# A hand-written order of 1,700 units of work: loads of two batches reordered, 19 sums on the other engine, a third of the units moved

## The chip, the cores and the metric

The kernel runs on one core of a Trainium2 chip. Its engines are named as in the profile: PE (TensorE: matmuls; PEld is its weight load), DVE (VectorE), ACT (ScalarE), POOL (GpSimd) and SP (SyncE, which here only issues stores). The metric is the device time of one execution in microseconds (us). A measurement is the median of several runs.

## What is computed

The kernel is an attention with 32 memory slots followed by a bilinear feed-forward network. Cut to what matters:

```
q, k, v: (8 batches, 8 heads, 576 tokens, 64)      phi: (8, 8, 576, 32)
a     = softmax over tokens of phi
k_m   = a^T k        v_m = a^T v                    (32 slots x 64, per head)
attn  = softmax over slots of q k_m^T / 8
x     = attn v_m, heads side by side                (4608 tokens x 512)
out   = ((x w_a) * (x w_b)) w_out                   (d_ff = 1536)
```

All arrays are float32 outside; the matmuls inside take float16.

## The kernel before, in words

**What a batch goes through.** phi, k, v and q of a batch are loaded by DMAs that POOL issues (L152, L155, L158, L163), k, v and q being cast to float16 on the way. ACT takes exp of phi (L291); PE sums k and v over the slots (`kv`, L323); DVE scales them (`km`, L350 and L355); PE turns them round (`kvt`, L363). DVE transposes q (`qt`, L300); PE makes the scores (`sc`, L412), ACT their exp (`e`, L425). For batches 0 to 3 the softmax is normalised through logarithms (`den`, `nr`, L465 to L478; for batches 2 and 3 the product L478 is POOL's); for the others by transposing on DVE, summing and multiplying (`ed`, `sm`, `tn`, `ad`, L485 to L506; `tn0` on POOL). The weights w_a and w_b are folded into v_m (`v0a` to `v2b`, eight narrow matmuls each for 512 columns and one weight, L516) and copied from PSUM to SBUF (`x`, L548, mostly ACT). So x w_a is one product of `attn` with the folded weights `vab`.

**The up projection** of a batch is cut into 12 blocks of 128 columns (i) and two halves of 288 tokens (hf; for batch 1 the halves are 320 and 256). A unit `a{b}.{i}.{hf}` is two matmuls and ACT's copy of the result to `a_sb` (L727, L731); `b{b}.{i}.{hf}` is two matmuls and DVE's product of `a_sb` and the second result into `ht` (L727, L734). For some blocks of batches 5, 6 and 7 both halves are made together with seven products in place of eight (`P{b}.{i}.{k}`, one matmul each, L750, L755, L759, L777), with a last product `H` (on POOL) or `J` (on DVE) (L781). These need sums of the folded weights (`S`, L533) and of the attention (`T`, L541), each marked P or D for POOL or DVE.

**The down projection** takes two blocks of 128 tokens together, also in seven products of six matmuls each: 18 pairs of 42 steps `d` (one matmul each, L654). It needs four sums of `ht` per pair, `h{pair}.{y}` on POOL or `g{pair}.{y}` on DVE (L638). ACT takes three partial results (L661) and one output (L705), DVE adds the rest (L665), and SP stores (L644).

**PSUM** has eight banks. The class `Banks` (from L198) gives each new result the bank that was freed longest ago; PE has to wait until ACT or DVE has read the result that lay there.

**The order** is written out by hand in the string `PLAN` (L18 to L80), a list of units. The last loop of the kernel (L785 on) walks through it and issues each unit's instructions; a scheduler does not reorder them. Each engine runs its own instructions in the order of the list, and semaphores hold it where data or a buffer is missing. POOL therefore issues a load only after the sums that stand ahead of it in the list, but it may be far ahead of PE. `d3` means three steps; a load is a letter and a batch: `p` phi, `k`, `v`, `q`, and `wa`, `wb`, `o` for weights. `kv_sb` has two buffers, so batches 4 and 6 take the one of 2; q and phi have two buffers each.

Of the kernel before, what the change touches and what calls it, by code (L numbers as in the profile page):

```python
# [15 lines left out]


PLAN = """  # L18
wb0:256 0qt0 wa0:256 0qt3 wb256:512 0qt1 wa256:512 p1 0exp0 0exp1 F1 0ks0 0kt0 0ks1 0vs1 0vt1 0vs0 0vt0 M k1 F1
0hv0a 0s0 v1 0qt2 O 0kt1 0e0 F1 0s1 0e1 0hx0a0 0hx0a1 F2 0den10 0den01 0den11 0den00 wa512:1024 0hv0b 0hx0b0 0hx0b1  # L20
0hv1b 0nr01 0nr10 0hx1b1 0nr11 0nr00 0hv1a 0hx1a0 q1.0 wb512:1024 0hx1a1 F4 a0.0.1 1exp1 a0.0.0 b0.0.0 0hx1b0 a0.1.1
b0.0.1 1exp0 a0.3.1 b0.1.1 a0.3.0 a0.2.0 b0.3.1 b0.2.0 a0.2.1 b0.2.1 1kv a0.1.0 1km1 wa1024:1536 1km0 b0.3.0 q1.1
1kvt 0v1a 0x1a0 0x1a1 1v0a 1v1a 1v0b 1x1a0 1x0a0 1x0b0 a0.5.1 1x1a1 1qh20 wb1024:1536 b0.1.0 o1 a0.6.0 1qh30 a0.4.0
1qh10 1qh00 o0 o3 1sh0 1eh00 0v1b 1v1b 1x0b1 1eh10 1x0a1 0x1b0 1den00 0x1b1 1x1b1 o4 1den10 o2 a0.6.1 b0.6.0 b0.6.1
b0.5.1 1nr10 1nr00 1x1b0 b0.4.0 a0.7.1 b0.7.1 a0.7.0 a0.5.0 b0.7.0 a1.5.0 b0.5.0 h0.3 b1.5.0 a1.3.0 1qh21 a0.4.1 o5
b1.3.0 1qh31 1qh01 a1.4.0 b0.4.1 a1.1.0 1qh11 a1.2.0 b1.4.0 a1.0.0 b1.1.0 1sh1 0v2a 1eh01 1eh11 0x2a1 b1.0.0 0x2a0
b1.2.0 1den01 a1.6.0 0v2b 0x2b0 0x2b1 b1.6.0 v2 a0.9.1 1v2b 1v2a 1x2b0 1x2b1 a0.11.1 1x2a1 1x2a0 b0.9.1 a0.10.1
a0.9.0 b0.11.1 b0.10.1 b0.9.0 V20 1den11 a1.10.0 b1.10.0 a0.11.0 b0.11.0 a0.8.0 a1.11.0 b0.8.0 b1.11.0 1nr11 d1
1nr01 a0.10.0 d1 V00 a1.8.0 b0.10.0 a1.7.0 d1 b1.8.0 p2 V21 a1.11.1 b1.7.0 b1.11.1 d1 a1.3.1 a1.0.1 a1.2.1 g0.0 d1
b1.3.1 a1.6.1 d1 b1.2.1 b1.0.1 V01 a0.8.1 V10 a1.4.1 a1.9.0 d1 k2 2exp0 2exp1 g0.1 d1 V11 b1.6.1 V31 a1.5.1 p3 g0.2  # L30
b0.8.1 q2 d1 b1.4.1 d3 a1.1.1 b1.9.0 d6 2kv 3exp0 k3 d2 2km0 d1 a1.9.1 2km1 v3 d3 b1.5.1 d1 3exp1 d1 a1.10.1 d2
a1.8.1 2kvt b1.1.1 d2 h1.0 a1.7.1 2qt1 d4 2qt0 2qt3 2v1b 2x1b1 2v0a 2x1b0 T30 2qt2 2x0a1 d12 2x0a0 d4 g2.0 g1.1 2sc
# [6 lines left out]
a2.2.1 d1 q5 d1 4qt0 b2.11.1 4qt3 4exp1 d1 3x0b1 d3 b2.2.1 d1 a2.9.1 d1 4qt1 d2 4qt2 d1 a2.7.1 b2.9.1 g4.3 d1 a2.6.1
h4.0 a2.3.1 d1 g4.1 d1 a3.3.0 d1 h4.2 4exp0 k7 b2.7.1 a3.2.0 d2 b2.6.1 d5 b3.3.0 b3.2.0 d2 4kv p6 3v2a 4km0 d2 3x2a1  # L40
4km1 d11 3x2a0 b2.3.1 d2 4kvt d2 a3.0.0 a3.3.1 v6 5km0 q6 d2 a3.1.0 5km1 k6 h5.0 d5 b3.1.0 a3.1.1 4sc 4e0 b3.0.0 d1
5qt3 d2 b3.1.1 5qt0 d1 a3.0.1 4e1 d3 b3.3.1 d5 3v1b 3v1a 4ed 3v2b 3x1b1 d5 3x1a0 d2 3x1a1 4sm0 d1 5qt1 d2 h5.3 3x2b0
5kvt a3.8.0 4sm1 d1 3x1b0 h5.1 3x2b1 d4 5qt2 d3 a3.6.1 b3.0.1 a3.10.0 d3 a3.4.0 d1 p7 d1 6exp1 d1 b3.8.0 b3.4.0 d1
a3.5.0 b3.6.1 d1 b3.10.0 4tn1 a3.7.0 a3.9.0 h5.2 d1 5sc 4tn0 5e0 d1 b3.5.0 5e1 a3.5.1 a3.11.0 d1 b3.7.0 d3 6qt0 d4
4v0a 4x0a0 4v1b 4v0b 4x0b1 d2 4x1b1 d5 6qt2 d1 4ad d1 5ed d1 a3.4.1 5sm0 b3.5.1 d2 b3.9.0 d1 4x1b0 d3 4x0a1 b3.11.0
d2 q7 d3 6qt1 d1 a3.6.0 a3.2.1 h6.3 6exp0 b3.6.0 d2 b3.4.1 d2 4x0b0 a3.8.1 a3.7.1 d5 a3.11.1 d2 b3.11.1 b3.8.1 d1
5tn0 d2 b3.2.1 4v2b 4v2a 4x2b0 6kv h6.0 4v1a d2 4x2b1 d1 5sm1 4x2a0 6km1 6km0 h6.1 6qt3 d3 b3.7.1 4x1a1 d3 4x1a0
a3.9.1 d2 4x2a1 5tn1 d2 b3.9.1 d3 a3.10.1 a4.0.0 g6.2 a4.2.1 b3.10.1 b4.0.0 d1 a4.3.0 d2 a4.0.1 6kvt b4.2.1 a4.6.0
d5 5ad 5v1a 6sc 5x1a1 h7.3 d1 6e1 d1 5x1a0 d1 7qt0 b4.6.0 d1 6e0 b4.0.1 d6 5T0D d2 h7.0 5v1b 5v0a 5v0b 5x1b0 g7.1
g8.0 g8.3 5x1b1 5T1D g7.2 5x0a0 d3 5x0b0 d6 5x0a1 b4.3.0 d8 5S01D a4.9.1 5T3D v7 a4.7.0 g8.1 b4.7.0 a4.10.1 a4.8.0  # L50
d1 b4.9.1 d1 5x0b1 a4.1.1 d2 5S11D 5S31P b4.8.0 b4.10.1 6ed 5S21P a4.6.1 a4.11.0 d1 b4.6.1 a4.5.0 d1 P5.4.1 7exp0
b4.5.0 b4.11.0 d1 b4.1.1 d3 P5.5.1 P5.4.2 a4.2.0 P5.5.2 d3 5S00P a4.1.0 d1 7qt3 5T2P P5.4.6 a4.9.0 h8.2 d1 a4.4.0
6sm0 d1 P5.5.5 b4.2.0 d1 7exp1 d1 6tn0 d1 b4.9.0 P5.4.5 P5.4.7 d1 P5.5.6 d3 P5.5.3 d1 a4.8.1 d2 b4.1.0 d1 5S10P d1
P5.4.3 P5.4.4 a4.4.1 a4.7.1 5S20P b4.4.1 d2 b4.4.0 d1 b4.8.1 5v2a 7qt2 5v2b 5x2a0 P5.5.7 5x2b0 b4.7.1 d4 5x2a1 6sm1
a4.10.0 a4.3.1 b4.3.1 d2 5x2b1 P5.5.4 P5.1.1 a4.11.1 b4.10.0 h9.3 d1 6tn1 d6 5S30D a4.5.1 d1 P5.2.1 P5.1.6 d1 J5.5
g9.0 a5.10.1 d1 P5.1.5 P5.2.2 d1 b4.11.1 d1 H5.4 h9.1 P5.1.7 d3 P5.1.2 d1 P5.2.5 d2 P5.2.6 d2 P5.1.3 P5.6.1 d1
P5.1.4 d1 P5.2.3 a5.11.0 d1 P5.2.7 d2 P5.7.1 a5.8.0 h9.2 d1 b4.5.1 P5.7.5 P5.6.6 P5.2.4 d3 P5.7.6 d1 P5.6.5 d1
P5.6.2 H5.1 P5.7.3 H5.2 d5 h10.0 P5.7.2 P5.6.7 a5.8.1 P5.3.1 P5.7.7 P5.6.3 b5.11.0 P5.0.1 d3 h10.1 d2 P5.6.4 P5.0.5
P5.3.6 P5.7.4 d1 b5.10.1 P5.0.6 d3 a5.9.0 6ad H5.7 d2 H5.6 P5.0.3 P5.3.2 d1 P5.3.5 d3 P5.0.2 d1 P5.3.7 d2 P5.0.7 d1
h10.3 a5.10.0 d1 P5.3.3 d3 6T0P d1 P5.3.4 d1 P5.0.4 d1 6T1P 6v0a 6x0a0 6x0a1 6T2P 7qt1 7kv 6v2b 6v0b H5.0 7km0 d1  # L60
H5.3 d1 6x2b1 d1 7km1 d4 6x0b0 6x0b1 d1 b5.8.0 6x2b0 d2 6T3P a5.11.1 b5.10.0 7kvt d1 b5.9.0 d3 6S00P d2 6v1a 7sc
6S10D d3 6x1a0 d1 7e1 d1 g11.0 6S30D g10.2 7e0 b5.8.1 6x1a1 d1 b5.11.1 d6 6v2a 7v1a 6v1b 6x2a1 g11.1 d1 6x1b0 6S20D
d2 6x1b1 d4 7ed 7sm0 a5.9.1 d4 6x2a0 d1 b5.9.1 7x1a1 P6.3.1 d7 6S01P d1 P6.3.2 d1 7x1a0 a6.11.0 7sm1 d1 P6.3.5
P6.3.6 d1 h11.2 d2 P6.1.1 d2 P6.1.2 d2 6S11P d1 b6.11.0 a6.8.0 P6.3.3 P6.1.6 P6.3.7 P6.1.5 d1 a6.10.0 d3 P6.2.5 d3
g12.0 6S31P P6.2.1 7tn1 d1 6S21D g11.3 P6.1.3 d4 H6.3 P6.1.7 P6.0.1 d3 P6.2.6 P6.3.4 d1 P6.2.3 d3 P6.0.6 d4 P6.2.2
P6.1.4 P6.2.7 d1 P6.0.5 d3 a6.10.1 d1 H6.1 P6.0.7 d2 P6.6.1 h12.1 d2 P6.2.4 d1 P6.0.3 P6.0.2 P6.6.5 H6.2 d4 h12.2
P6.6.6 d1 7tn0 P6.0.4 b6.8.0 P6.5.1 d2 H6.0 d2 P6.6.3 P6.6.7 d1 a6.9.0 H6.6 P6.6.2 d2 P6.5.6 d1 P6.5.2 P6.4.1
b6.10.0 P6.5.5 P6.6.4 d3 P6.5.7 d1 h12.3 7ad P6.4.5 d1 P6.4.6 d1 P6.5.3 P6.7.1 P6.4.2 d3 P6.5.4 d4 7T2P d1 7T0P
P6.7.6 P6.4.7 P6.4.3 P6.7.5 H6.5 d3 P6.7.2 d4 P6.4.4 d1 H6.4 d1 h13.3 d1 P6.7.3 P6.7.7 7v0a 7v1b 7x0a0 d2 7x1b1
b6.9.0 d1 7x0a1 d2 7x1b0 d1 P6.7.4 d2 7T1D a6.8.1 7S01D g13.0 7S11D a6.11.1 d1 7T3D d1 g13.1 7v0b 7x0b1 J6.7 7v2a  # L70
7v2b 7S21D g13.2 7x2a0 d2 7x2b1 d11 P7.4.1 d3 P7.4.2 7x0b0 b6.10.1 d5 7x2a1 7S31D 7S00D d2 7x2b0 d3 7S10P b6.11.1 d1
P7.4.6 a7.8.0 d2 P7.4.5 d2 b6.8.1 a6.9.1 P7.4.7 P7.7.1 P7.7.5 P7.4.3 d1 b7.8.0 b6.9.1 a7.11.0 d1 P7.4.4 P7.7.6 d1
a7.10.0 P7.7.3 d2 P7.5.1 P7.7.2 d1 7S30P d1 P7.7.7 P7.5.5 d2 H7.4 b7.10.0 P7.5.2 P7.5.6 h14.0 P7.6.1 d2 P7.7.4
a7.9.0 d1 P7.5.3 d2 P7.5.7 d1 J7.7 d1 g14.1 d1 P7.6.6 d1 P7.1.1 P7.6.5 P7.6.2 d1 7S20P d1 h14.2 P7.5.4 d3 P7.6.7
H7.5 d1 b7.11.0 P7.1.6 d1 h14.3 P7.1.5 P7.6.3 d1 P7.1.2 d2 P7.6.4 d1 P7.0.1 d1 P7.1.7 d1 H7.6 d1 b7.9.0 d1 P7.0.5 d1
P7.0.2 d1 P7.1.3 P7.0.6 d2 P7.1.4 P7.2.1 d2 P7.0.3 P7.3.1 d3 P7.0.7 P7.2.2 P7.2.6 P7.3.5 d3 P7.3.6 d2 J7.0 P7.2.5
P7.0.4 d1 H7.1 P7.2.7 d1 a7.10.1 P7.3.7 d5 P7.3.2 d2 P7.2.4 d3 P7.3.4 g15.0 d1 a7.8.1 d3 a7.9.1 g15.1 a7.11.1
# [764 lines left out]
```

## Time and profile before

| | us |
|---|---|
| median of 3 runs | 234.23 |
| lowest and highest run | 233.62 to 234.96 |
| span of the profiled execution, first to last instruction | 232.1 |
| busy in it: PE, DVE, ACT, POOL | 214.1, 195.7, 169.4, 138.2 |

The profile gives of the profiled execution only its span; the runs include what lies around it as well. The TensorE clock was granted in full (1.000). The views used below are: the windows (busy time of each engine in a stretch), the waits (who waited for whom), the timeline of one engine, the chain of work that ended last, the groups of equal instructions, and the DMA issues with their time to landing. Start times count from the start of the span.

### The profile page before, as it was taken

The page shows a single profiled execution, that of the slowest core. Times are in us where ns is not written, and L with a number is a line of the kernel's source. Part 1 is how long each engine was busy: PE and PEld are TensorE (multiplying, and loading weights), DVE is VectorE, ACT ScalarE, POOL GpSimd, SP SyncE. Part 2 cuts the span into 40 slices and gives each one's busy share as a digit, 9 for nine tenths or more (in the row PEclk, how much of TensorE's full clock was granted, in tenths as well). Part 3 has the DMA queues.
Part 4 walks back from the last instruction along what each step waited for, and adds up shares of the span by engine and source line. Part 5 has one row for each costly group of instructions (what it writes and reads, how often), then busy time and mean ns, then how long its engine had stood idle before and what let it go on. Part 6 is the DMA issues. An engine that isn't in the chain of part 4 may idle for free.

```text
span 232.1 us, 7493 instructions
## 1 busy us (share of the span) xinstructions
PE 214.1 (92%) x2906; PEld 163.6 (70%) x2906; DVE 195.7 (84%) x517; ACT 169.4 (73%) x450; POOL 138.2 (60%) x139
## 2 busy tenths in 40 slices
...
GB/s 229 238 199 256 205 205 205 205 259 258 208 284 138 264 207 243 253 241 254 210 93 4 190 1 65 28 64 32 93 3 90 78 16 92 18 77 55 42 158 111
DMA packets 26259, 34.09 MB, mean 147 GB/s; under 512 B 2000, under 2 KB 20304, under 8 KB 26224
## 3 DMA queue, kind: packets, MB, share of 16 engines
...
q1 hardware_dynamic: 5952, 9.70, 16.2%
q10 hardware_dynamic: 512, 0.79, 1.0%
...
q14 instruction: 13, 0.11, 0.1%
...
## 4 chain that ended last, share of the span: by engine, by line
PE 71%; DMA 17%; POOL 6%; ACT 3%; issue 2%; DVE 1%; POOLq 0%
PE py L654 18%; PE pb L727 11%; PE pa L727 11%; PE pv L654 9%; DMA wb_sb<-in_moe_w_b_dram 6%; DMA kv_sb<-in_k_dram 6%; PE py L750 5%; PE px L654 4%; PE pva L516 4%; DMA kv_sb<-in_v_dram 4%; PE pv L750 3%; POOL h_sums L638 2%; PE pkv L323 2%; PE px L750 1%; ACT vab L548 1%
## 5 line engine op out<-in xcount | busy, mean ns | idle before, releaser
L734 DVE TENSOR_TENSOR ht<-a_sb,pb 128x288 f16<-128x288 f16 (+2 forms) x144 | 60.5, 445 | 9.6 <-PE pb L727 5.3
L727 PEld LDWEIGHTS <-vab 128*128 128x128 f16 x576 | 55.3, 98 | 14.9 <-issue 2.4
L731 ACT CAST a_sb<-pa 128x288 f16<-128x288 f32 (+2 forms) x144 | 55.1, 417 | 13.6 <-PE pa L727 8.9
L727 PE MATMUL pb<-A,vab 128*128 128x288 f16 (+2 forms) x288 | 54.9, 286 | 0.1
L727 PE MATMUL pa<-A,vab 128*128 128x288 f16 (+2 forms) x288 | 54.3, 286 | 0.5 <-DVE A L478 0.4
L548 ACT CAST vab<-pva 128x512 f16<-128x512 f32 x82 | 45.4, 611 | 6.9 <-PE pva L516 6.8
L654 PEld LDWEIGHTS <-h_sums 128*128 128x128 f16 x432 | 41.4, 98 | 9.9 <-issue 2.4
L638 POOL TENSOR_TENSOR h_sums<-ht 128x768 f16<-128x768 f16 x19 | 31.2, 1645 | 21.4 <-DVE ht L734 21.3
L654 PE MATMUL py<-w_sums,h_sums 128*128 128x256 f16 x216 | 38.1, 273 | 0.0
L654 PEld LDWEIGHTS <-ht 128*128 128x128 f16 x324 | 31.2, 98 | 7.5 <-issue 2.2
L654 PE MATMUL pv<-wo_sb,h_sums 128*128 128x256 f16 x216 | 36.4, 273 | 0.0
L638 POOL TENSOR_TENSOR h_sums<-ht,h_sums 128x768 f16<-128x768 f16 x10 | 16.4, 1640 | 11.6 <-DVE h_sums L638 11.5
L755 ACT COPY z<-py 128x288 f32<-128x288 f32 x48 | 19.2, 415 | 2.3 <-PE py L750 1.8
L781 POOL TENSOR_TENSOR ht<-ah,bh 128x288 f16<-128x288 f16 x19 | 13.7, 737 | 10.1 <-DVE ah L759 7.1
L654 PE MATMUL px<-wo_sb,ht 128*128 128x256 f16 x108 | 18.9, 273 | 0.0
L654 PE MATMUL py<-wo_sb,ht 128*128 128x256 f16 x108 | 18.8, 273 | 0.0
L654 PE MATMUL py<-w_sums,ht 128*128 128x256 f16 x108 | 18.4, 273 | 0.0
L661 ACT ACTIVATE u<-py 128x256 f32<-128x256 f32 x36 | 14.4, 399 | 4.0 <-PE py L654 3.9
L425 ACT ACTIVATE E<-pscore 128x288 f16<-128x288 f32 x28 | 9.8, 431 | 9.5 <-PE pscore L412 9.4
L291 ACT ACTIVATE exp_sb<-phi_sb 128x576 f16<-128x576 f32 x16 | 10.9, 692 | 5.2 <-DMA phi_sb<-in_phi_dram 5.2
L300 DVE STREAM_TRANSPOSE qT<-q_sb 128x288 f32<-128x288 f32 x28 | 12.2, 456 | 2.6 <-DMA q_sb<-in_q_dram 2.6
L750 PE MATMUL py<-asum,vab 128*128 128x288 f16 x48 | 13.5, 286 | 0.0
...
## 6 DMA issues: line engine op xcount, KB each, us to landing
...
phi_sb<-in_phi_dram POOLq DMA_DIRECT2D x8, 576.0 KB, 10.3
kv_sb<-in_v_dram POOLq DMA_DIRECT2D x8, 576.0 KB, 11.2
kv_sb<-in_k_dram POOLq DMA_DIRECT2D x7, 576.0 KB, 13.5
q_sb<-in_q_dram POOLq DMA_DIRECT2D x6, 576.0 KB, 11.9
wo_sb<-in_moe_w_out_dram POOLq DMA_DIRECT2D x6, 256.0 KB, 14.0
wa_sb<-in_moe_w_a_dram POOLq DMA_DIRECT2D x2, 512.0 KB, 14.2
...
```

Source lines behind the costliest of these rows:

```text
L291: nc.scalar.activation(out=t["exp"][:, 2 * z:2 * z + 2, :, :], in_=phis[b][:, 2 * z:2 * z + 2, :].rearrange("p c (i m) -> p c i m", m=M), ...
L300: nc.vector.transpose(out=t["qT"][:, hp, :].bitcast(F32), in_=qs[b][:, hp, :].bitcast(F32))
L548: engine_copy(out=vabs[b][z][:, g, lo:hi], in_=pva[:, 0:hi - lo])
L638: engine.tensor_tensor(out=out, in0=in0, in1=in1, op=op)
L654: nc.tensor.matmul(po, lhs[:, i], rhs[:, i], start=first and i == 0, stop=i == KH - 1, skip_group_check=not first)
L661: nc.scalar.mul(out=x, in_=po, mul=scale)
L727: nc.tensor.matmul(ps, vabs[b][x][:, g, P * i:P * (i + 1)], attn[b][:, g, ts], start=(g == 0), stop=(g == 1))
L731: nc.scalar.copy(out=a_sbs[b, i, hf][:, :n], in_=ps)
L734: nc.vector.tensor_tensor(out=ht[:, i, t0:t0 + n], in0=a_sbs.pop((b, i, hf))[:, :n], in1=ps, op=ALU.mult)
L750: nc.tensor.matmul(x[bank][0], lhs, rhs, start=first, stop=True, skip_group_check=True)
L755: nc.scalar.copy(out=x[name], in_=po)
L781: engine.tensor_tensor(out=ht[:, i, t0 + HALF:t0 + S], in0=x["ah"], in1=x["bh"], op=ALU.mult)
```

## The change

Only the string `PLAN` changes; no code does. The list has the same units but for the engine of 19 sums, and its first 195 units, each step `d` counted, (to about 49 us) are the same. Behind them:

- **Loads.** The order of issue on POOL from phi of batch 2 on was `p2 k2 p3 q2 k3 v3 q3 p5 v5 p4 k5 q4 v4 k4 q5 k7 p6 v6 q6 k6 p7 q7 v7` and is `p2 k2 p3 q2 v3 k3 q3 p5 q4 p4 k5 v5 v4 k4 q5 p6 q6 p7 k6 v6 k7 q7 v7`.
- **Sums moved from DVE to POOL** (11): g3.1, g4.1; 5S11, 5S30; 5T0, 5T1, 5T3, 7T1; J5.5, J7.0, J7.3.
- **Sums moved from POOL to DVE** (8): h2.2, h3.2, h17.2, h17.3; 5T2, 7T2; H5.4, H6.4.
- **Places.** About a third of the 1,500 units behind the first eighth stand more than 1 us of PE's work earlier or later than before, some 230 of them more than 2 us; the steps `d` stand in fewer and longer groups.

The diff where POOL's loads of batches 3, 5 and 4 stand, and at the end of the list:

```diff
-g1.2 2e0 b1.7.1 d1 2e1 g1.3 q3 d2 b1.8.1 d3 b1.10.1 d1 2den0 d1 g2.1 p5 2den1 d1 b1.9.1 d1 2nr0 d5 2v2b 3kv 2v1a
-g2.3 2x2b1 3km0 2nr1 2x2b0 2x1a1 d7 3km1 d6 3qt2 2x1a0 2v0b 2v2a 2x0b1 3qt3 d3 3qt0 2x2a1 d3 a2.6.0 d1 b2.6.0 d1
-3qt1 a2.4.0 2x2a0 b2.4.0 d1 h2.2 d1 a2.7.0 d2 a2.4.1 d1 2x0b0 b2.4.1 d4 a2.3.0 a2.1.1 3kvt 5exp1 v5 b2.7.0 p4 b2.3.0
-a2.8.0 b2.1.1 k5 a2.1.0 d2 a2.2.0 d2 q4 d1 a2.5.0 h3.3 3sc 3e0 d2 b2.2.0 d1 3e1 d2 b2.8.0 5exp0 d1 b2.1.0 v4 d2
-a2.10.0 d2 b2.10.0 a2.0.1 a2.11.0 b2.11.0 b2.5.0 3den0 a2.0.0 d1 b2.0.1 h3.0 d1 g3.1 a2.5.1 d1 a2.9.0 k4 b2.5.1 h3.2
...
+b1.5.1 a1.4.1 d7 T30 d2 2kv 3exp0 a1.8.1 d3 q3 d1 2km0 d1 2km1 b1.9.0 3exp1 b1.4.1 d2 a1.10.1 d2 a1.9.1 p5 d2 2kvt
+b1.1.1 d1 2qt1 d1 2qt3 d2 a1.7.1 2qt0 2v0a 2x0a0 2v1b 2x1b0 2qt2 d5 2x1b1 d6 b1.10.1 d2 2x0a1 d2 g1.1 d1 2sc 2e0
+b1.7.1 2e1 b1.9.1 d1 q4 d2 g1.2 d5 2den0 g2.0 d3 2den1 g1.3 2nr1 2nr0 d3 g2.3 2v2b 3kv 3km1 3km0 2x2b0 2v1a d6 2x1a0
+d3 p4 d2 2x1a1 d1 k5 d3 v5 2x2b1 2v2a 2x2a0 3qt0 2v0b 2x0b0 2x2a1 v4 b1.8.1 d2 h3.0 h3.1 a2.6.0 d4 b2.6.0 a2.7.0 g2.1
+2x0b1 a2.4.0 b2.4.0 a2.9.0 b2.9.0 a2.5.0 b2.5.0 d1 3qt3 a2.5.1 d2 a2.3.0 d1 a2.1.1 d3 b2.7.0 5exp1 b2.3.0 a2.10.0
+b2.1.1 d2 a2.2.0 h3.3 3qt2 d1 3qt1 d2 5exp0 d1 b2.10.0 a2.4.1 b2.5.1 3kvt a2.0.0 g2.2 a2.8.0 b2.8.0 d3 g3.2 3sc 3e0 k4
...
-b7.11.1 b7.9.1 d12 g15.2 g15.3 P7.2.3 b7.8.1 P7.3.3 d12 b7.10.1 d1 J7.3 H7.2 g16.0 d7 g16.1 g16.2 g16.3 g17.0 g17.1
-d2 h17.2 d20 h17.3 d66
...
+b7.9.1 d2 g15.3 P7.2.3 P7.3.3 d2 a7.11.1 d5 b7.8.1 d1 H7.2 d7 H7.3 d17 b7.11.1 g16.0 d9 g16.1 g16.2 d11 g16.3 g17.3
+d28 g17.0 d11 g17.1 d1 g17.2 d32
```

More of the change, by code (lines that the diff above doesn't have):

```diff
@@ L18 @@
 PLAN = """
[L19 to L32, printed above, removed]
-g1.2 2e0 b1.7.1 d1 2e1 g1.3 q3 d2 b1.8.1 d3 b1.10.1 d1 2den0 d1 g2.1 p5 2den1 d1 b1.9.1 d1 2nr0 d5 2v2b 3kv 2v1a
@@ L39 @@
[L39 to L77, printed above, removed]
-b7.11.1 b7.9.1 d12 g15.2 g15.3 P7.2.3 b7.8.1 P7.3.3 d12 b7.10.1 d1 J7.3 H7.2 g16.0 d7 g16.1 g16.2 g16.3 g17.0 g17.1
```

51 lines of the change are left out of this document (50 added, 1 removed).

## The prediction

> **What bounds the kernel now.** I read the windows first, since shares over the whole span mix the start with the rest. Columns: stretch, its length, then busy time (instructions) of PE, PEld, DVE, ACT, POOL, the granted clock, DMA share and GB/s.
>
> ```profile
> 40.00:60.00 20.00, 20.00 (x290) 15.00 (x293) 19.82 (x54) 16.77 (x48) 9.70 (x12) 1.00 1.20 237
> 80.00:100.00 20.00, 19.41 (x343) 15.46 (x342) 15.69 (x46) 15.35 (x40) 16.00 (x14) 1.00 1.19 232
> 140.00:160.00 20.00, 20.00 (x184) 16.28 (x183) 19.59 (x52) 15.66 (x45) 16.48 (x15) 1.00 0.24 55
> 180.00:200.00 20.00, 20.00 (x202) 15.97 (x201) 19.53 (x53) 15.92 (x44) 14.68 (x16) 1.00 0.24 55
> ```
>
> From 40 us on PE is busy all the time at clock 1.00, except 0.59 us between 80 and 100 (the stretches left out read 20.00 too). DVE is nearly full too from 140 on, with no time to make up a delay. The waits, asked for PE alone and 40 to 228 us, give one row, and PE's timeline shows its place:
>
> ```profile
> PE pkv L323 <- DMA kv_sb<-in_k_dram: 0.6, 1, 0.6
> 91.32 0.38 PE L654 MATMUL py<-w_sums,h_sums 128*128 128x256 f16 x2
> 92.30 0.94 PE L323 MATMUL pkv<-kv_sb,exp_sb 64*32 64x192 f16 x72 [0.59 <-DMA kv_sb<-in_k_dram]
> ```
>
> This is unit 4kv, waiting for the last load of batch 4, k4. Busy rows can hide small gaps, as one matmul's record overlaps the next, so I also set PE's order against its pitch, from the chain:
>
> ```profile
> 190.99 0.49 PE pa L727 x4
> 191.70 0.77 PE pva L516 x24
> 218.12 1.31 PE py L654 x12
> 49.27 0.43 PE L727 MATMUL pb<-A,vab 128*128 128x320 f16 x2
> 227.30 0.81 PE L654 MATMUL py<-w_sums,ht 128*128 128x256 f16 x6
> ```
>
> A step d (one matmul) is 1.31/12 = 0.109 us, an up half (two matmuls) 0.49/2 = 0.245, a fold of eight 0.77/3 = 0.26 with its share of the change to narrow tiles. Laid along the list from the first moved unit's place (49.27) to the start of the last matmul (227.30 + 5 x 0.109 = 227.84), such pitches give about 177.4 us; the trace took 178.57. So all that any order could gain behind the first eighth is about 1.2 us. The wait for k4 is 0.59 of it as idle time, or 0.76 counted from where the next matmul was due (91.32 + 2 x 0.109 = 91.54), which holds the change to narrow tiles that every order pays; I take 0.65. The first 49 us are the same instructions in both lists.
>
> **The change, part by part.** The span is 232.1 us and the median of the runs 234.23, so 2.1 us lie around the span; I keep them and add to 234.23.
>
> *PE's work.* Each list holds the same matmuls (2906) and, by my count, the same 21 stretches of narrow tiles behind the first eighth: 0 us. Only waits can change the time.
>
> *Loads.* POOL issues them in its own order, between sums:
>
> ```profile
> 60.60 0.76 POOL L152 DMA_DIRECT2D phi_sb<-in_phi_dram  x1
> 66.77 2.52 POOL L478 TENSOR_TENSOR A<-E,vsum 128x576 f16<-128x576 f16 x2 [5.40 <-ACT vsum L476]
> 69.25 1.63 POOL L638 TENSOR_TENSOR h_sums<-ht,h_sums 128x768 f16<-128x768 f16 x1
> 70.84 0.79 POOL L158 DMA_DIRECT2D kv_sb<-in_v_dram  x1
> 71.62 0.77 POOL L152 DMA_DIRECT2D phi_sb<-in_phi_dram  x1
> 77.85 0.77 POOL L155 DMA_DIRECT2D kv_sb<-in_k_dram  x1
> 70.00:72.00 2.00, 2.00 (x19) 1.66 (x18) 1.79 (x5) 1.76 (x6) 2.00 (x3) 1.00 0.58 133
> 78.00:92.00 14.00, 13.70 (x193) 10.86 (x190) 10.80 (x27) 12.71 (x33) 9.25 (x8) 1.00 1.19 223
> ```
>
> After p5 (60.60) POOL issues nothing for 10 us, because v5 stands behind the products of batch 2's normalising (L478) and sum h2.2. The transfers run dry (share 0.58 at 70 to 72), then stay full until k4 lands. k4's issue at 77.85 took this long, and p4's (71.62) this:
>
> ```profile
> kv_sb<-in_k_dram POOLq DMA_DIRECT2D x1, 576.0 KB, 14.3
> phi_sb<-in_phi_dram POOLq DMA_DIRECT2D x1, 576.0 KB, 8.5
> ```
>
> So p4 landed at 80.1 and k4 at 92.2; k5, q4, v4, k4 followed p4, four loads in 12.1 us, 3.0 each. In the new list q4 stands right behind p5, ahead of L478, and goes out at about 62 (its buffer is free once batch 2's q is transposed), into the dry stretch. h2.2 moves to DVE, so p4 follows L478 at 66.77 + 2.52 = 69.3, then k5 70.1, v5 70.8, v4 71.6; after three sums of 1.64 k4 goes out at about 77.3, hardly earlier. But now p4 leads: it lands no later than 69.3 + 8.5 = 77.8, and k5, v5, v4, k4 at 3.0 each by 80.8, 83.8, 86.8 and 89.8. On PE's pitch 4kv comes at the same place as before (91.4), so k4 is some 1.6 us early: **-0.65 us**, between 0.59 and 0.76. What is late next: 5kv, 0.4 us earlier in the list (at 83.9), needs v5, which my late bound gives 83.8. With p4 landing sooner (its queue is empty, so I expect 76) v5 lands at 82. Price 0, up to 0.3.
>
> The later loads q6, p7, k6, v6 move back: q6 now waits for 4qt0 (8.4 us later in the list), so v6 leaves near 100. The slowest v of before took this long (least, median, most):
>
> ```profile
> DMA to landing us min/median/max: 5.8/11.2/18.0
> ```
>
> Even so v6 lands by 118, and 6kv stands at 118.5: 0 us.
>
> *Sums.* By engine:
>
> ```profile
> L638 POOL TENSOR_TENSOR h_sums<-ht 128x768 f16<-128x768 f16 x19 | 31.2, 1645 | 21.4 <-DVE ht L734 21.3
> L781 POOL TENSOR_TENSOR ht<-ah,bh 128x288 f16<-128x288 f16 x19 | 13.7, 737 | 10.1 <-DVE ah L759 7.1 <-PE py L750 2.5 <-PE py L654 0.5
> L533 POOL TENSOR_TENSOR vsum<-vab 128x512 f16<-128x512 f16 x3 | 3.4, 1150 | 5.0 <-DVE vab L533 5.0
> L638 DVE TENSOR_TENSOR h_sums<-ht 128x768 f16<-128x768 f16 x17 | 9.2, 549 | 0.1
> L781 DVE TENSOR_TENSOR ht<-ah,bh 128x288 f16<-128x288 f16 x5 | 1.5, 298 | 0.0
> L533 DVE TENSOR_TENSOR vsum<-vab 128x512 f16<-128x512 f16 x3 | 1.2, 416 | 0.0
> ```
>
> Eleven go to POOL: 2 h (1.64), 2 S (1.15), 4 T and 3 H (0.74 each, T being of H's size): +10.8 us there, -4.0 us on DVE. Eight go to DVE: 4 g (0.55), 2 T and 2 J (0.30): +3.4 on DVE, -9.5 on POOL. Net -0.6 us on DVE, +1.2 on POOL: nothing, unless a sum comes late where it is used. The closest such places: g17.0 to g17.2 now stand right ahead of the last pair, behind DVE's last sum of pair 16, three times 0.55 us against steps of PE 6 x 0.109 apart; I count 0.2 us of room at each. h14.2 and h14.3, 1.64 us each on POOL, have about 0.1. Together 0 to 0.4 us; I take 0.1.
>
> *Moved units.* Each PSUM bank can be written again only when ACT or DVE has read it:
>
> ```profile
> L731 ACT CAST a_sb<-pa 128x288 f16<-128x288 f32 x120 | 46.3, 418 | 10.5 <-PE pa L727 8.1 <-ACT z L755 0.7
> L734 DVE TENSOR_TENSOR ht<-a_sb,pb 128x288 f16<-128x288 f16 x120 | 50.8, 446 | 9.6 <-PE pb L727 5.3 <-ACT a_sb L731 1.2 <-PE px L654 0.8
> ```
>
> I went through both lists with the kernel's own rotation of eight banks. Of 462 reuses behind the first eighth, 30 come within 1.2 us of PE time after the reading unit's place before, 58 after. Such a reading takes 0.42 to 0.45 us. The 30 of before cost nothing (no such wait in PE's list), so the nearest row says 0; the other end is one reader too late, 0.45, at perhaps one in six of the 28 new ones, 2 us. DVE and ACT run 0 to 0.3 us closer to these banks around 71 to 73, 86, 113, 125, 135 and 197 to 204 us. I take 0.2.
>
> **Sum:** 234.23 - 0.65 + 0.1 + 0.2 = **233.9 us**.
>
> **The rivals.**
>
> *Nothing new waits* (20%): 234.23 - 0.65 = 233.6. For it: the whole of before shows that banks used again within 1.2 us need not cost.
>
> *Banks hold PE up* (other side, 11%): DVE or ACT falls behind where readings crowd, as after 70 us, where five up-half pairs of batch 2 follow closely beside g2.1 and a fold's copy, and at 134 and 200. The price is 0.45 per late reader. It decides from about 1.8 us, four late readers; with six, 234.23 - 0.65 + 2.7 = 236.3. Against it: the new list has no reuse under 0.68 us, the old one went down to 0.44.
>
> *POOL's sums hold DVE up* (10%). DVE's and POOL's timelines:
>
> ```profile
> 174.88 0.45 DVE L759 TENSOR_TENSOR bh<-py,z 128x288 f16<-128x288 f32 x1
> 175.24 0.55 DVE L638 TENSOR_TENSOR h_sums<-ht 128x768 f16<-128x768 f16 x1
> 175.71 0.68 DVE L502 TENSOR_TENSOR E<-E,sum 128x512 f16<-128x512 f16 x1
> 176.31 0.41 DVE L533 TENSOR_TENSOR vsum<-vsum,vab 128x512 f16<-128x512 f16 x1
> 176.64 0.55 DVE L638 TENSOR_TENSOR h_sums<-ht 128x768 f16<-128x768 f16 x1
> 177.34 1.42 POOL L781 TENSOR_TENSOR ht<-ah,bh 128x288 f16<-128x288 f16 x2 [2.48 <-PE py L750]
> ```
>
> H6.3's second operand was there at 175.3; it began only when four DVE sums in a row were done. Laid side by side, none of DVE's 38 sums of L638 stands beside a sum of POOL. So the two exclude each other, and the other way round a DVE sum that meets a POOL sum just begun waits up to 1.64 us, with every bank reading behind it. The new list puts 5S11P close to g8.1 and g8.3 (at 131) and H6.3 to g11.3 (at 174). If two such meetings cost PE 1.3 us each, 234.23 - 0.65 + 2.6 = 236.2. Against it: 4 us less of sums on DVE means fewer meetings, and before shows no DVE wait on POOL. [...]
>
> *The load order doesn't do what it says* (7%): q4 goes out late, k4 still lands after 91.4. The 0.6 stays: 234.23 + 0.3 = 234.5.
>
> **How the numbers follow.** The forecast has 52%. Half a per cent, about what a measurement of this kernel can tell from no change, is 1.17 us: 233.06 and 235.40. Faster than that would need nearly all of the 1.2 us that PE loses now: 6%, from scatter around the first two cases. Slower holds most of the two cases on that side and a little of the forecast: 19%. The rest, 75%, is no difference. The range runs from 233.0 (the whole 1.2 gained) to 235.6 (2 us lost to banks, 0.65 gained), leaving out most of the two slow cases.
>
> **What would show it.** PE's waits from 40 us on without the row for in_k_dram; k4 landing before 91; POOL issuing q4 before its two L478 products; PE busy 20.00 in every 20 us. Against me: new waits of PE on ACT a_sb, DVE ht or h_sums; idle DVE just ahead of a sum, ended as a POOL sum ends; a wait of 5kv for in_v_dram. The span should read 231.8.

## The result and the profile after

The changed kernel takes 236.02 us (median of 6 runs, 235.35 to 237.00); the kernel before, run beside it, 233.91 us (6 runs, 233.35 to 234.96). The ratio is 1.0092, with a 95% interval of 1.0065 to 1.0119: slower by 0.9%, and above the range. The profiled execution of the changed kernel took 236.3 us. Its page begins:

```profile
span 234.6 us, 7504 instructions
PE 215.2 (92%) x2906; PEld 163.6 (70%) x2906; DVE 198.9 (85%) x514; ACT 170.1 (72%) x450; POOL 141.0 (60%) x142
```

The span is 2.5 us longer than before's 232.1, with the same 2906 matmuls. The windows of the changed kernel (same columns as in the prediction) show where PE is not full:

```profile
40.00:60.00 20.00, 19.08 (x274) 14.01 (x272) 19.73 (x49) 16.17 (x45) 10.47 (x12) 1.00 1.20 237
80.00:100.00 20.00, 20.00 (x349) 16.22 (x347) 14.09 (x41) 16.65 (x45) 11.53 (x11) 1.00 0.88 176
120.00:140.00 20.00, 19.30 (x297) 15.15 (x274) 18.15 (x45) 17.34 (x44) 13.74 (x12) 1.00 0.60 112
160.00:180.00 20.00, 19.74 (x306) 15.43 (x304) 18.62 (x48) 17.26 (x45) 12.94 (x14) 1.00 0.23 54
```

The 0.59 us lost between 80 and 100 is gone. In its place 0.92, 0.70 and 0.26 us are lost in three stretches that were full (and 0.12 between 60 and 80). The clock stays at 1.00. PE's waits between 40 and 231 us say for whom:

```profile
PE pb L724 <- DVE ht L731: 0.9, 1, 0.9
PE pa L724 <- DVE ht L731: 0.7, 1, 0.7
PE py L747 <- DVE ht L774: 0.3, 1, 0.3
```

(Lines of the changed kernel are 3 lower than before's.) No row names a load any more; all three name a bank that DVE had not yet read. POOL's timeline and the record of k4's issue show the loads:

```profile
63.51 0.75 POOL L160 DMA_DIRECT2D q_sb<-in_q_dram  x1 [2.40 <-PE pb L724]
68.22 2.51 POOL L475 TENSOR_TENSOR A<-E,vsum 128x576 f16<-128x576 f16 x2 [3.96 <-ACT vsum L473]
70.68 0.79 POOL L149 DMA_DIRECT2D phi_sb<-in_phi_dram  x1
78.65 0.78 POOL L152 DMA_DIRECT2D kv_sb<-in_k_dram  x1
kv_sb<-in_k_dram POOLq DMA_DIRECT2D x1, 576.0 KB, 11.7
```

q4 is issued ahead of the two L475 products, as forecast, and k4 lands at 78.65 + 11.7 = 90.3, ahead of its use. Everything on POOL is some 1.4 us later than forecast, for a reason that comes now.

**The first of the three waits**, DVE, then POOL, then PE:

```profile
55.66 0.54 DVE L635 TENSOR_TENSOR h_sums<-ht,h_sums 128x768 f16<-128x768 f16 x1
56.13 1.99 DVE L618 TENSOR_TENSOR w_sums<-wo_sb,w_sums 128x768 f16<-128x768 f16 x1
58.04 0.41 DVE L731 TENSOR_TENSOR ht<-a_sb,pb 128x256 f16<-128x256 f16 x1
55.82 1.88 POOL L635 TENSOR_TENSOR h_sums<-ht 128x768 f16<-128x768 f16 x1 [8.35 <-DVE ht L731]
57.15 0.43 PE L724 MATMUL pb<-A,vab 128*128 128x320 f16 x2
58.51 0.38 PE L724 MATMUL pb<-A,vab 128*128 128x256 f16 x2 [0.92 <-DVE ht L731]
```

The sum V31 (L618) takes 1.99 us; the same form takes 0.54 in the row above it. POOL's h1.0 became ready at 55.82, while DVE's g0.2 was under way. It did its 1.64 us of work between the two DVE sums, and V31 stood until it was done. The reading of a bank at 58.04 was queued behind V31, and PE behind that: after 57.15 the next matmul was due at 57.43 and came at 58.51, 1.08 us late. Another 0.28 follows at 61.1; 0.09 of it is a change to narrow tiles, which took as much ahead of two folds of batch 2 in before's trace, where nothing waits (59.76 + 0.109 = 59.87 to 59.96), so the first wait costs 1.27 in all.

**The second**, same order of rows:

```profile
132.28 0.55 DVE L635 TENSOR_TENSOR h_sums<-h_sums,ht 128x768 f16<-128x768 f16 x1
132.75 1.51 DVE L635 TENSOR_TENSOR h_sums<-ht 128x768 f16<-128x768 f16 x1
132.51 1.33 POOL L530 TENSOR_TENSOR vsum<-vab 128x512 f16<-128x512 f16 x1 [3.12 <-DVE vab L530]
134.15 0.49 PE L651 MATMUL pv<-wo_sb,h_sums 128*128 128x256 f16 x3
135.34 0.41 PE L724 MATMUL pa<-A,vab 128*128 128x288 f16 x2 [0.70 <-DVE ht L731]
```

5S11, one of the sums moved to POOL, slips in between g8.1 and g8.3; g8.3 takes 1.51 us. PE was due at 134.15 + 3 x 0.109 = 134.48 and came at 135.34: 0.86 us.

**The third:**

```profile
177.58 1.22 DVE L499 TENSOR_TENSOR E<-E,sum 128x512 f16<-128x512 f16 x1
177.47 0.78 POOL L778 TENSOR_TENSOR ht<-ah,bh 128x288 f16<-128x288 f16 x1 [1.56 <-DVE h_sums L635]
179.04 0.38 PE L651 MATMUL py<-w_sums,h_sums 128*128 128x256 f16 x2
179.69 0.28 PE L747 MATMUL py<-A,vab 128*128 128x288 f16 x1 [0.26 <-DVE ht L774]
```

Here H6.3 on POOL gets in ahead of 7tn1 (L499), which takes 1.22 us in place of 0.68. PE loses 179.69 - 179.26 = 0.43, and 0.11 at 181.7. A fourth sum is drawn out without harm: g2.2 (moved to DVE) takes 0.74 us at 78.39 beside POOL's h3.3 (77.07 to 78.71), and PE does not wait there. In before's trace no sum of DVE is drawn out in this way: L638's 38 take 0.535 to 0.559 us, and L502's four 0.675 to 0.685.

To compare kernels without the scatter of start and end I use one number, *PE's path*: from the first moved unit's place to the start of the last matmul. For the changed kernel:

```profile
49.21 0.43 PE L724 MATMUL pa<-A,vab 128*128 128x320 f16 x2
229.71 0.81 PE L651 MATMUL py<-w_sums,ht 128*128 128x256 f16 x6
```

229.71 + 5 x 0.109 - 49.21 = **181.04 us**; before's is 178.56 by the same two places. The 2.48 us between them are the slowdown.

### The profile page after: what moved, and what is told of

It reads as the page before. It is cut to its first block, busy times and chain, and to the rows that moved or that the text cites. A ratio compares the mean times of both kernels' runs of the same rounds, so it can differ in the third digit from the quotient of the medians.

```text
span 234.6 us, 7504 instructions
## 1 busy us (share of the span) xinstructions
PE 215.2 (92%) x2906; PEld 163.6 (70%) x2906; DVE 198.9 (85%) x514; ACT 170.1 (72%) x450; POOL 141.0 (60%) x142
## 4 chain that ended last, share of the span: by engine, by line
PE 79%; DMA 10%; DVE 6%; POOL 2%; issue 1%; DVEq 0%; POOLq 0%
PE py L651 20%; PE pb L724 14%; PE pa L724 13%; PE pv L651 9%; DMA wb_sb<-in_moe_w_b_dram 6%; PE pva L513 5%; PE py L747 5%; PE px L651 5%; DMA kv_sb<-in_v_dram 4%; PE pv L747 2%; PE pkv L320 2%; DVE ht L731 1%; PE px L747 1%; DVE w_sums L618 1%; PE pscore L409 1%
## 5 line engine op out<-in xcount | busy, mean ns | idle before, releaser
L728 ACT CAST a_sb<-pa 128x288 f16<-128x288 f32 (+2 forms) x144 | 56.0, 415 | 15.9 <-PE pa L724 8.7
L724 PE MATMUL pa<-A,vab 128*128 128x288 f16 (+2 forms) x288 | 55.7, 286 | 1.1 <-DVE ht L731 0.7
L635 POOL TENSOR_TENSOR h_sums<-ht 128x768 f16<-128x768 f16 x18 | 30.0, 1671 | 20.4 <-DVE ht L731 20.1
L651 PE MATMUL py<-w_sums,h_sums 128*128 128x256 f16 x216 | 35.6, 273 | 0.0
L651 PE MATMUL pv<-wo_sb,h_sums 128*128 128x256 f16 x216 | 35.1, 273 | 0.0
L778 POOL TENSOR_TENSOR ht<-ah,bh 128x288 f16<-128x288 f16 x20 | 14.4, 734 | 11.1 <-DVE ah L756 8.4
L651 PE MATMUL py<-wo_sb,ht 128*128 128x256 f16 x108 | 19.4, 273 | 0.0
L651 PE MATMUL px<-wo_sb,ht 128*128 128x256 f16 x108 | 18.1, 273 | 0.0
L651 PE MATMUL py<-w_sums,ht 128*128 128x256 f16 x108 | 17.6, 273 | 0.0
L635 POOL TENSOR_TENSOR h_sums<-h_sums,ht 128x768 f16<-128x768 f16 x7 | 11.5, 1640 | 5.1 <-DVE h_sums L635 4.7
```

The costliest lines, as they stand in the source:

```text
L635: engine.tensor_tensor(out=out, in0=in0, in1=in1, op=op)
L651: nc.tensor.matmul(po, lhs[:, i], rhs[:, i], start=first and i == 0, stop=i == KH - 1, skip_group_check=not first)
L724: nc.tensor.matmul(ps, vabs[b][x][:, g, P * i:P * (i + 1)], attn[b][:, g, ts], start=(g == 0), stop=(g == 1))
L728: nc.scalar.copy(out=a_sbs[b, i, hf][:, :n], in_=ps)
L778: engine.tensor_tensor(out=ht[:, i, t0 + HALF:t0 + S], in0=x["ah"], in1=x["bh"], op=ALU.mult)
```

## The experiments

Theory 1: the loads gain 0.65 us; what costs is three meetings, a POOL sum that goes ahead of a waiting DVE sum, with bank readings queued behind it. Rivals: the moved units lose time at the banks by themselves, or the moving of the sums as a whole costs. Diffs show the changed pieces of the list only. Ratios are to the kernel before, run in the same rounds; they are not the plain quotient of the medians. Its median was 234.66 us beside the first four experiments, 234.71 beside the next four and 233.82 beside the last four, with single runs from 233.2 to above 236, so a difference of a few tenths of a per cent between rounds means little; the paths carry the account.

**Moving the sums apart in the changed kernel.** `part_first` puts V31 ahead of h1.0:

```diff
-b0.8.1 h1.0 g0.2 V31
+g0.2 V31 b0.8.1 h1.0
```

> The changed kernel with one edit: on DVE the sums g0.2 and V31 stand ahead of b0.8.1 again, so that POOL's sum h1.0, which waits for b0.8.1, is released only when they are done. PE's order is the same. Theory 1 (a POOL sum released between two DVE sums takes its place ahead of the second, and PE then waits for banks that DVE has not read): V31 takes 0.55 us in place of 1.99, PE's wait at 57 us (1.08 in pitch) and the following one at 61 us (0.28) go, 236.0 - 1.3 = 234.7 us. Theory 2 (the banks are used again too soon wherever readings crowd, whatever POOL does): V31 may get shorter, but PE waits at the same places, within 0.3 us of 236.0.

Measured: 236.34 us, ratio 1.0068 (1.0039 to 1.0097), PE's path 180.62. V31 took 0.56 us, but the expectation missed: b0.8.1's bank is now read about 1 us later, and PE waits 0.28 and 0.53 us at 57 in place of 1.27. The place is tight whichever goes first. The second and third waits stayed.

`part_second` moves g8.3 away from 5S11:

```diff
-b4.6.0 5S01D g8.1 ... 5S31P d1 g8.3
+b4.6.0 g8.3 5S01D g8.1 ... 5S31P d1
```

> The changed kernel with one edit: on DVE g8.3 stands ahead of 5S01D in place of behind 5S31P, so that only g8.1 and no second sum is in line on DVE when 5S01D releases POOL's 5S11P. PE's order is the same. Theory 1: g8.3 takes 0.55 us in place of 1.51, PE's wait at 134 us (0.86 in pitch) goes, 236.0 - 0.9 = 235.1 us. Theory 2: the wait stays, 236.0 within 0.3 us.

Measured: 234.80 us, ratio 1.0031 (0.9999 to 1.0063), path 178.94. The wait at 134 is gone, as expected. But the first wait was gone too, though nothing there was edited: V31 took 0.55 us and h1.0 2.35.

`part_all` has both edits and moves g11.3 and H6.3 behind 7tn1 and g12.0:

```diff
-b6.11.0 g11.3 d1 P6.1.5 H6.3 6S21D a6.8.0 d2 P6.2.5 7tn1 d2 g12.0
+b6.11.0 d1 P6.1.5 6S21D a6.8.0 d2 P6.2.5 7tn1 d2 g12.0 g11.3 H6.3
```

> The changed kernel with the edits of both other parts and a third: g11.3 and, behind it, H6.3 stand behind g12.0, so that POOL's H6.3, which may write ht only when g11.3 has read it, is released when DVE's four sums are done. Theory 1: V31, g8.3 and 7tn1 take 0.55, 0.55 and 0.68 us, PE's waits at 57, 61, 134 and 179 us go (1.08 + 0.28 + 0.86 + 0.43 = 2.65 in pitch), 236.0 - 2.65 = 233.4 us, at or a little below the kernel before. Theory 2: 236.0 within 0.5 us. If the moved sums cost by themselves (DVE and POOL carry other loads than before), something between: 234.5 to 235.5.

Measured: 234.81 us, ratio 1.0011 (0.9983 to 1.0039), path 179.26. V31, g8.3 and 7tn1 all had their usual durations, and of the waits only the 0.28 and 0.53 us that the first edit brought, 0.18 at 188 and 0.14 at 52 remain. Without these 1.13 us the path is 178.13. (PE's row for the 0.53, at 57.48, names a DMA of q. By ACT's timeline it is a bank: ACT's reading L657 ends at 57.42, and ACT had stood 0.93 us for b0.8.1 just before.)

**Bringing a meeting into the kernel before.** `meet_in_before` moves one product there:

```diff
-b1.6.1 V31 a1.5.1 p3 g0.2 b0.8.1
+b1.6.1 b0.8.1 V31 a1.5.1 p3 g0.2
```

> The kernel before with one edit: b0.8.1 stands ahead of V31 and g0.2, so that POOL's h1.0 is released while V31 runs and g0.2 is still in line on DVE. Its loads, its other sums and the rest of its order are those of before. Theory 1: g0.2 takes about 1.5 to 2.0 us in place of 0.55, and PE waits some 0.5 to 1.1 us near 57 us: 233.9 + 0.8 = 234.7 us. Theory 2: no change, 233.9 within 0.3 us, because its banks are as far apart as before.

Measured: 234.21 us, ratio 0.9973 (0.9944 to 1.0002), path 178.18. A miss. POOL's timeline shows that this time POOL stood:

```profile
56.15 2.35 POOL L636 TENSOR_TENSOR h_sums<-ht 128x768 f16<-128x768 f16 x1 [8.75 <-DVE ht L732]
```

h1.0 needs 1.64 us and shows 2.35: it waited for both DVE sums, V31 and g0.2. So the theory's rule was too strict. A POOL sum that is ready while one DVE sum runs and another is next in line may get in between, or not. The path is shorter than before's for another reason: the first 49 us took 0.4 us longer here while k4 landed at 92.2 as before, so PE waited for it 0.2 us in place of 0.6.

**The loads alone.** `loads_in_before` is the kernel before with one load moved:

```diff
-g2.1 p5 2den1 ... a2.2.0 d2 q4 d1 a2.5.0
+g2.1 p5 q4 2den1 ... a2.2.0 d2 d1 a2.5.0
```

> The kernel before with one edit: the load q4 is issued right behind p5, ahead of POOL's products of batch 2, as in the changed list. Every sum and every other unit stays. Theory 1 (the loads gain what was forecast, the meetings of sums lose it): PE's wait for in_k_dram (0.59 us idle) goes and nothing comes in its place; the last matmul starts at 227.84 - 0.65 = 227.2 us, and the time falls by 0.65 us, ratio 0.997. Rival (the gain is given back at the next wait): the last matmul stays at 227.8.

Measured: 233.70 us, ratio 0.9955 (0.9922 to 0.9988), path 177.91. PE's waits between 40 and 231 us are empty. q4's and k4's issues on POOL, k4's time to landing and PE's first matmul on it:

```profile
62.30 0.75 POOL L161 DMA_DIRECT2D q_sb<-in_q_dram  x1 [0.58 <-DVE qT L298]
77.47 0.78 POOL L153 DMA_DIRECT2D kv_sb<-in_k_dram  x1
kv_sb<-in_k_dram POOLq DMA_DIRECT2D x1, 576.0 KB, 11.3
91.98 0.94 PE L321 MATMUL pkv<-kv_sb,exp_sb 64*32 64x192 f16 x72
```

k4 lands at 88.8, 3.2 us ahead of its use. The loads gain 178.56 - 177.91 = 0.65 us, and 177.91 is what PE needs with no wait. The last matmul starts at 227.5, not 227.2, as 0.34 us were lost ahead of the first moved unit. As `meet_in_before` shows, a later start alone shortens the wait for k4, so the 0.65 holds for a start like before's. By its median this is the fastest kernel of the study, ahead of both.

**A meeting made by hand.** `meet_mid` is `loads_in_before` with g4.3 moved beside POOL's h4.0:

```diff
-4qt3 4exp1 d1 3x0b1 d3 b2.2.1 ... b2.9.1 g4.3 d1 a2.6.1
+4qt3 4exp1 d1 3x0b1 g4.3 d3 b2.2.1 ... b2.9.1 d1 a2.6.1
```

> The kernel loads_in_before with one more edit: DVE's sum g4.3 stands ahead of b2.2.1 in place of behind b2.9.1, so that DVE comes to it while POOL is in the middle of h4.0. PE's order is the same, DVE's work is the same. Theory 1: g4.3 takes up to 1.5 us in place of 0.55, b2.2.1 is read some 1 us later than the bank is wanted, PE waits 0.6 to 1.0 us on DVE near 88.5 us, and the kernel is 0.6 to 1.0 us slower than loads_in_before. Theory 2 (POOL's sums don't hold DVE up; only the crowding of bank readings counts): g4.3 takes 0.55 us, DVE is at most 0.5 us later, no wait of PE.

Measured: 234.80 us, ratio 1.0008 (0.9979 to 1.0037), path 178.70. DVE's g4.3, POOL's h4.0, and PE:

```profile
87.77 1.47 DVE L636 TENSOR_TENSOR h_sums<-ht 128x768 f16<-128x768 f16 x1
87.16 1.65 POOL L636 TENSOR_TENSOR h_sums<-ht 128x768 f16<-128x768 f16 x1
88.86 0.41 PE L725 MATMUL pa<-A,vab 128*128 128x288 f16 x2
89.65 0.41 PE L725 MATMUL pa<-A,vab 128*128 128x288 f16 x2 [0.39 <-DVE ht L732]
```

One DVE sum placed under a POOL sum costs 178.70 - 177.91 = 0.79 us (0.55 of it at 89.65, 0.27 at 90.7), in a kernel in which nothing else is moved. That is the price of a meeting, shown by itself: theory 1 holds.

**The race.** `changed_again` is the changed kernel unedited.

> The changed kernel once more, unedited, beside the others on the same chip, to see whether each of its three meetings goes the same way again. Theory 1 with POOL's sum always ahead of the second DVE sum: V31 1.99, g8.3 1.51, 7tn1 1.22 us again, last matmul at 230.25 us. If the first meeting is a race that either side may win (part_second had the same list there and V31 took 0.55): V31 0.55 or 1.99 us, last matmul at 228.9 or 230.25 us.

Measured: 235.27 us, ratio 1.0033 (1.0007 to 1.0059), path 179.79. DVE's V31 and POOL's h1.0 this time:

```profile
56.14 0.56 DVE L618 TENSOR_TENSOR w_sums<-wo_sb,w_sums 128x768 f16<-128x768 f16 x1
55.84 2.35 POOL L635 TENSOR_TENSOR h_sums<-ht 128x768 f16<-128x768 f16 x1 [8.53 <-DVE ht L731]
```

POOL came at nearly the same moment as in the first profile (0.17 against 0.16 us after g0.2's start) and had to wait. So the first meeting goes either way in one and the same program, and is worth 181.04 - 179.79 = 1.25 us. In this run q4 is issued at 62.1, p4 at 69.4 and k4 at 77.4, and k4 lands at 89.9, each within 0.2 us of the forecast. In all, the changed list's order of these three sums was profiled five times (here, in the first profile, in `part_second`, `one_sum_back` and `sums_back`); DVE stood once. The second and third meetings were the same in both profiles of the unedited list: waits of 0.7 and 0.3 us. Measured again, the list is 0.3% slower than before, where the first measurement had 0.9%.

`repaired` has the edits of `part_second` and the third meeting, and for the first another order:

```diff
-b1.6.1 b0.8.1 h1.0 g0.2 V31 a1.5.1
+b1.6.1 V31 b0.8.1 h1.0 g0.2 a1.5.1
```

> The changed kernel with g8.3 ahead of 5S01D and g11.3, H6.3 behind g12.0 as in part_all, but with V31 alone ahead of b0.8.1 (g0.2 stays behind it), so that only one DVE sum follows h1.0's release and b0.8.1 comes 0.5 us earlier than in part_all. Theory 1: no sum of DVE but g2.1 and g2.2 is drawn out, the waits of 0.28 and 0.53 us that part_all had at 57 us shrink to 0.3 at most, the last matmul starts at 227.5 to 227.9 us, the ratio to before is 0.998 to 1.000. Theory 2: no better than part_all (228.46 us).

Measured: 234.23 us, ratio 0.9985 (0.9958 to 1.0011), path 179.25, with 0.39 us lost at 57 (0.3 at most was expected), 0.18 at 188, 0.14 at 52, and 0.45 at 129, which is new. DVE's transpose of batch 7's q, then PE's folds, which take 0.61 us in `part_all`:

```profile
128.39 0.48 DVE L296 STREAM_TRANSPOSE qT<-q_sb 128x288 f32<-128x288 f32 x1 [0.64 <-DMA q_sb<-in_q_dram]
129.31 1.06 PE L512 MATMUL pva<-wb_sb,kvT 64*32 64x512 f16 x16
```

The new list issues q7 14 us later than before (118.99 for 105.06). It landed 10.5 us ahead of its use in before's trace, 0.6 in the changed kernel's first, and here DVE stood for it, with the bank readings behind. The three meetings away, the changed list is level with before in time, as the forecast had it; by its path it is still 0.7 us longer than before, so its small waits use up what the loads gain. The last matmul starts at 229.0, 1.1 us later than expected; 0.5 of this arose ahead of the first moved unit, the rest is among these waits.

**Sums put back, and one moved.** `one_sum_back` is the changed kernel with one engine letter undone, 5S11P to 5S11D.

> The changed kernel with one of the 19 sums, 5S11, back on DVE; its place in the list stays. Theory 1 (a DVE sum behind which a POOL sum slips in is held for all of POOL's sum): 5S21P can only start once 5S11 is done, so it finds g8.3 under way and DVE has no further sum in line; g8.3 takes 0.55 us again, and PE's 0.9 us wait at 134 is gone. From the first moved unit's place to the start of the last matmul: 180.2 us if the first meeting (V31 with h1.0) is lost again, 178.9 if it is won; the wait at 177 stays. Rival (the readers of the banks are too dense at 134 whatever the sums do): a wait of 0.5 us or more stays there. Ratio 0.999 to 1.005.

Measured: 234.70 us, ratio 1.0031 (1.0006 to 1.0056), path 179.28. DVE's 5S11 and g8.3, POOL's 5S21, and PE:

```profile
131.60 0.42 DVE L529 TENSOR_TENSOR vsum<-vab 128x512 f16<-128x512 f16 x1
131.94 0.55 DVE L634 TENSOR_TENSOR h_sums<-ht 128x768 f16<-128x768 f16 x1
132.11 1.40 POOL L529 TENSOR_TENSOR vsum<-vsum,vab 128x512 f16<-128x512 f16 x1 [3.85 <-DVE vsum L529]
133.00 0.49 PE L650 MATMUL pv<-wo_sb,h_sums 128*128 128x256 f16 x3
133.57 0.40 PE L723 MATMUL pa<-A,vab 128*128 128x288 f16 x2
```

g8.3 takes 0.55 us, POOL's next sum waits for it, and PE loses 133.57 - 133.33 = 0.24 in place of 0.86. One letter out of 19 was worth 0.6 us here. The path is 0.4 us longer than forecast for a won race: 0.24 remained here and 0.17 is new at 152.

`sums_back` puts all 19 sums on their old engines, at their new places.

> The changed kernel with all 19 sums back on the engines that they had before; loads and places stay changed. Theory 1: of the three meetings only the second (g8.3, at 131) came from the sums' engines, so it goes; the first (V31 with h1.0, a race) and the third (7tn1 with H6.3, 0.4 us of PE's time) came from moved units and stay. First moved unit to last matmul 179.9 to 180.3 with the race lost, 178.8 to 179.2 won. Rival (the move of sums as a whole is what costs): no sum of DVE drawn out and 178.0 to 178.5. Ratio 0.998 to 1.005.

Measured: 246.93 us (4 runs), ratio 1.0535 (1.0461 to 1.0608), path 189.92. Both expectations missed widely. POOL's h3.0, DVE's g3.1 and PE, then windows:

```profile
73.33 3.25 POOL L634 TENSOR_TENSOR h_sums<-ht 128x768 f16<-128x768 f16 x2
75.03 1.98 DVE L634 TENSOR_TENSOR h_sums<-h_sums,ht 128x768 f16<-128x768 f16 x1 [4.20 <-POOL h_sums L634]
77.43 0.41 PE L723 MATMUL pb<-A,vab 128*128 128x288 f16 x2 [4.45 <-DVE ht L730]
74.00:76.00 2.00, 0.00 (x0) 0.00 (x0) 0.97 (x1) 0.00 (x0) 2.00 (x2) 1.00 1.06 299
78.00:80.00 2.00, 2.00 (x12) 1.36 (x11) 1.33 (x4) 1.19 (x3) 2.00 (x2) 0.57 1.20 223
80.00:82.00 2.00, 2.00 (x11) 1.34 (x10) 0.91 (x2) 1.27 (x4) 1.89 (x2) 0.58 1.21 208
82.00:84.00 2.00, 2.00 (x21) 1.68 (x20) 1.91 (x5) 1.60 (x5) 0.41 (x1) 1.00 1.21 210
```

g3.1 reads what h3.0 writes, and the new list has h3.0 behind four loads on POOL and the next sum right behind it. On POOL the two follow each other; with g3.1 on DVE, DVE and all bank readings stand for 4.2 us, and PE for 4.45. Behind that the granted clock read 0.57 and 0.58 in two windows of 2 us, by my estimate some 1.7 us more (2 x 0.43 + 2 x 0.42). Two meetings are there as well. 7tn1 takes 1.22 us beside H6.3 as in the changed kernel, so the third meeting does come from moved units. At 156.16 a product of DVE (L777) takes 1.59 us for 0.30 beside a POOL sum that began at 155.94, and PE waits 1.47 us. So places and engines of the new list belong together, and this run can't say what the sums alone cost.

`first_on_dve` makes h1.0 a sum of DVE:

```diff
-b0.8.1 h1.0 g0.2 V31
+b0.8.1 g1.0 g0.2 V31
```

> The changed kernel with one sum, h1.0, made by DVE (0.55 us) in place of POOL (1.64 us), so that V31 has no POOL sum beside it. Theory 1: V31 takes 0.55 us, no wait of PE at 57 to 61; the meetings at 131 and 177 stay with 0.9 and 0.4 us; first moved unit to last matmul 179.7, ratio 1.003. Rival (DVE is simply too full at 55 to 58): 0.55 us more on DVE there holds PE up as much as before, 180.5 or more, ratio 1.007.

Measured: 237.15 us (4 runs), ratio 1.0117 (1.0070 to 1.0163), path 180.75. It came out at the rival's figure, but not for its reason: with h1.0 gone, POOL reached T30, its next sum, earlier, and that met g1.0. DVE, POOL, PE:

```profile
55.96 1.19 DVE L634 TENSOR_TENSOR h_sums<-ht 128x768 f16<-128x768 f16 x1
54.85 1.89 POOL L617 TENSOR_TENSOR w_sums<-wo_sb,w_sums 128x768 f16<-128x768 f16 x1 [7.32 <-DVE w_sums L617]
57.67 0.72 PE L650 MATMUL pv<-wo_sb,h_sums 128*128 128x256 f16 x5 [0.71 <-DVE h_sums L634]
```

`no_meeting` adds to it the edits of the second and third meeting.

> The changed kernel without its three meetings: h1.0 made by DVE, g8.3 moved ahead of 5S01D (5 places), g11.3 and H6.3 moved behind 7tn1 and g12.0. Theory 1: no sum of DVE drawn out by more than 0.2 us behind 55 us, no wait of PE of 0.3 us or more; first moved unit to last matmul 178.3, with small waits of the moved units 0.2 to 0.5 over the floor of 177.9; ratio 0.996 to 0.999, so no slower than before and level with the forecast. Rival (the moved units lose time at the banks by themselves): 179.0 or more with waits on ACT's or DVE's readings of 0.3 us each, ratio 1.000 to 1.003.

Measured: 235.35 us, ratio 1.0044 (1.0014 to 1.0074), path 179.39. The waits at 134 and 177 are gone, the new meeting of g1.0 with T30 is there again (1.19 us) and is PE's only listed wait, 0.7 us. The expectation missed, since the edit brought in a fourth meeting.

## Why the prediction was wrong

The account of PE's path in the first profile closes: 177.91 with no wait, plus 1.08 + 0.19 (first meeting), 0.86 (second), 0.43 + 0.11 (third), and 0.13, 0.18, 0.06 and 0.06 in small waits of moved units, makes 181.01; measured 181.04. Before, 177.91 + 0.65 for k4.

- **PE's work at 0: right; the bound: too high.** Nothing but waits changed the time. "About 1.2 us" as the most that any order could gain was too much: the pitches gave 177.4 us, but without any wait PE took 177.91, so 0.65 was all there was.
- **Loads, -0.65: right.** By itself the moved load gave 0.65. Only the times of issue came later (q4 63.5 for 62, k4 78.65 for 77.3, landed 90.3 for 89.8), which the spare time covered. The later loads cost nothing in the first profile, but the list of those that move back left out q7; its spare time was nearly gone, and in `repaired` it cost 0.45.
- **Sums, +0.1: here it failed.** The step counted the work that moved ("net -0.6 us on DVE, +1.2 on POOL: nothing, unless a sum comes late where it is used") and looked for late sums only. No sum came late. What it left at nothing is what a sum does to the *other engine's next instruction*: three meetings, 1.27 + 0.86 + 0.54 = 2.67 us in the first profile, about 1.4 when the first goes the other way.
- **Moved units, +0.2 for banks: right in kind, half the size.** The small waits are 0.43 us. The term asked only how soon a bank is used again, not which sums come to stand side by side, and so missed the first and the third meeting. The rival "banks hold PE up" needs 1.8 us of such waits; beside the meetings there are these 0.43.
- **The rival "POOL's sums hold DVE up" happened**, at 236.2 us against 236.02, and was given 10%. It named g8.3 with 5S11 rightly; at 174 it named H6.3 with g11.3, where the sum that stood was 7tn1; V31 with h1.0 it did not see. The price of 1.3 us each was too high for the two that it named, 0.86 and 0.54; that the total came to its 2.6 is luck, as the unseen first meeting added 1.27. The other prices are 0.79 in `meet_mid` and 1.47 in `sums_back`. Its "4 us less of sums on DVE means fewer meetings" was the wrong measure, and only 0.6 net by the prediction's own sum: before had no meeting, with three more sums on DVE, since what counts is the place of each sum in the two queues. The first and third came from moved units, the second from one sum's change of engine.
- **One row was misread.** H6.3's late start in before (177.34) was put down to four DVE sums in a row. In the changed kernel's row the profile names DVE's h_sums, L635, as what H6.3 waited for: it overwrites a part of `ht` that g11.3 reads. The exclusion is real (g4.3 took 1.47 us for 0.55 in `meet_mid`), but it does not show there as idle time.
- **"Idle DVE just ahead of a sum"**, named as what would show the rival, was the wrong sign: there is none. The waiting sum is drawn out instead.

That the median rose by 2.1 us and the first profile by 2.5 would fit a first meeting that is lost in some executions only; single timed executions have no trace, so this is argued, not shown.
